# Four 32-row groups instead of two 64-row halves for the query-key sums of a linear-attention and gated-MLP block

## The chip, the cores and the metric

The kernel runs on one core of one Trainium2 chip. The metric is the device time of one execution in microseconds (us); several executions are timed and their median is given. One further kind of execution is recorded by the hardware profiler, and all views of the profile come from it. The engines are PE (matmul; PEld are its weight loads), DVE (vector), ACT (scalar), POOL (GpSimd) and SP, which here issues most DMAs.

## The reference

Input `x` is 2048 rows of 640. The rows are normalised (mean and variance over 640), and the result `xn` goes through two branches whose outputs are added to `x`:

```python
# branch A: linear attention, 32 heads of width 20
q, k, v = split(xn @ wqkv)
pq, pk = q @ w_phi[h], k @ w_phi[h]                      # per head, 20 x 20
phi_q = concat(softmax(pq), softmax(-pq))                # 40 features a head
phi_k = concat(softmax(pk), softmax(-pk))
kv  = sum over rows of phi_k^T v                         # 40 x 20 a head
z   = sum over rows of phi_k
o   = (phi_q @ kv) / (phi_q . z + 1e-6)
A   = o @ wo
# branch B: gated MLP, F = 1536
B   = (silu(xn @ w1) * (xn @ w3)) @ w2
out = x + A + B
```

## The kernel before, in words

The rows are worked in 16 row tiles of 128 and in 4 chunks of 4 tiles. `h`eads lie 20 columns apart, so 640 columns are five groups of 128.

**Order of work.** Each step is an operation of a planner (`Plan`, lines 12 to 83): an engine, an estimated duration, what it depends on, which ring buffer it takes or frees. PE's operations keep the order of the code; for DVE, ACT, POOL and SP the planner picks, among the next 80 of each engine, the one that by its estimates can start first. The resulting order is written out once; on the chip each engine then runs its list in that order, held only by semaphores. Rings have fixed numbers of buffers; `bank` is six PSUM banks that all products share, `kv` two further banks, first the accumulators of the key sums and later buffers of the query-key sums.

**First part (to about 139 us).** `LN` normalises the rows of a chunk: POOL computes `rstd` (lines 316, 317) from the statistics of four tiles (lines 301, 305), DVE applies it tile by tile (line 347, `ln_apply`), SP stores `xn` and loads it back transposed as `xnT` (lines 381, 386). An apply or a statistic is pinned behind a given DVE instruction by `order_after`, so it can't run ahead of it. For chunks 2 and 3 `LN` is called at tiles 4 and 8; its four applies wait in the list `applies`, and each following call of `GU` takes one, pinned behind that call's `gs`. `K(t)` makes key features: two products (line 442), four exponentials on ACT (`ek`, line 488), the sums and reciprocals on DVE (`ks`, `kr`, lines 497 and 506), then `phik`, the positive half on DVE and the negative half on POOL (line 514). `V(t)` makes the values, `KV(t)` adds ten products of one tile to `kva` and `kvb` (line 533). `fill` places gated-MLP units `GU` between them: two products of five 512-column matmuls (line 611), `th` on ACT (627), `gs` on DVE (632), `up` on ACT (650), their product `hT` on POOL (655). A `bank` of the first product is free when `gs` is done.

**Hand-over.** After the last `KV`, `kv_evac` (lines 662 to 677) writes the masked sums into two tables `kvr[sgn]` with four DVE products of 64 rows and 420 elements (line 669): rows 0 to 63 hold the features of heads 0 to 15, rows 64 to 127 those of heads 16 to 31; a 64-row group touches four heads, 88 columns.

**Second part.** `Q(c, g)` makes the query products of a chunk (line 689) and both exponentials (`eq`, line 704). `RT` makes the query-key sums: for a row tile and one sign, five steps of two matmuls, one on rows 0 to 63 and one on rows 64 to 127 of the array, 88 columns each (line 743). Three such units form one run (`RT(b)`), eleven runs in all; a unit writes two banks, and two of three units use the `bank` ring. ACT copies them to `rt` (line 759). `ATT(pair)` turns two tiles into attention outputs on DVE (`m` to `ca`, lines 784 to 789; `om`, lines 805 and 815), `OT(pair)` stores them (`od`, line 837) and loads them transposed (`oT`, line 845). `O(t)` adds, for a row tile, `hT @ w2` (line 871) and `oT @ wo` (line 877) in one bank; DVE adds the input (`res`, line 889), SP stores the output (line 894). The runs 3 to 10 lie in the middle of a tile's w2 products.

Of the kernel before, what the change touches and what calls it, by code (L numbers as in the profile page):

```python
# [86 lines left out]
def kernel(  # L87
# [33 lines left out]
    h0 = [64 * j // Dh for j in range(10)]  # L121
    g0 = [P * g // Dh for g in range(NQ)]

    x2 = A_x[0]
# [30 lines left out]
    vaug = [acts.tile([P, H, Dh + 1], bf, name=f"vaug{i}") for i in range(4)]  # L155
    kvr = [acts.tile([P, NQ, 4 * HC], bf, name=f"kvr{i}") for i in range(2)]
    kva, kvb = (kvpool.tile([P, 512], f32, name=n, tag="kv", bufs=2) for n in ("kva", "kvb"))
# [45 lines left out]
    band2 = consts.tile([P, 20], bf, name="band2")  # L203
    mask = consts.tile([P, NQ, 4], bf, name="mask")
    hmask = consts.tile([P, NQ, GH], bf, name="hmask")
# [45 lines left out]
    def kv_constants():  # L251
        make_band(band2[0:64, :], 20)
        make_band(band2[64:128, :], 20)
        for g in range(NQ):
            b = 4 - (64 * g - Dh * h0[g]) // 4
            nc.gpsimd.tensor_copy(out=mask[:, g, :], in_=band2[:, b : b + 16 : 5])
        for kv in kvr:
            nc.gpsimd.tensor_copy(out=kv[:].rearrange("p g (h c) -> p g h c", c=HC)[:, :, :, HC - 1], in_=mask[:])
# [10 lines left out]

    plan = Plan(dict(bank=6, five=4, half=2, pair=4, rt=4, kv=2, th=3, gs=3, up=3, hT=3, big=4))  # L270

# [6 lines left out]
    def dve_us(n, x=1):  # L278
        return 0.065 + n / 960.0 / x
# [76 lines left out]

    applies = []

    def LN(c, k=None):

        ln_rstd(c)

        def al():
            xn[c] = five.tile([P, 4, D], bf, name="xn", tag="five")

        a = xn_of[c] = plan.alloc("five", al)
        if k is None:  # L370
            for i in range(4):
                applies.append(lambda k, i=i: ln_apply(4 * c + i, [a, pin_of[k]], k))
            applies.append(lambda k: LN_out(c, [apply_of[4 * c + i] for i in range(4)]))
        else:
            LN_out(c, [ln_apply(4 * c + i, [a, pin_of[k]], k) for i in range(4)])

    def LN_out(c, ds):
        a = xn_of[c]
        st = plan.op(
            "SP", 0.5,  # L380
            lambda: nc.sync.dma_start(out=xn_d[c][:].rearrange("(t p) d -> p t d", p=P), in_=xn[c][:]),
            deps=ds, frees=[a], lat=3.5,
        )

        def tr():
            pinned["xnT", c] = nc.sync.dma_start_transpose(
                out=xnT[:, :, 512 * c : 512 * c + 512], in_=xn_d[c][:]
            )

        xt = plan.op("SP", 0.5, tr, deps=[st], lat=5.0)  # L390
        for t in range(4 * c, 4 * c + 4):
            XT_of[t] = xt
# [78 lines left out]
    def K(t):  # L471
# [6 lines left out]
        def alp():  # L478
            phik_b[t] = work.tile([P, 10, 2, 64], bf, name="phik", tag="rt", bufs=4)

        ekb = plan.alloc("pair", al)
        pkb = phik_a[t] = plan.alloc("rt", alp)
        for half in range(2):
# [63 lines left out]
    def prep(key, wT, dst, after):  # L547
# [6 lines left out]
        def columns(c, side):  # L554
            if key == "q":
                return dst[:, c, :].rearrange("p (g s f) -> p g s f", s=2, f=64)[:, :, side, :]
            return dst[:, c, 320 * side : 320 * side + 320].rearrange("p (g f) -> p g f", f=64)

        wphi_ready[key] = []

        def unit(c, side):
            def add():
                o = {}

                def fn():
                    o["ps"] = bank([P, 320], f32)
                    for n, (g, at, width, col) in enumerate(FSPANS[side]):
# [9 lines left out]
                        "ACT", act_us(320),  # L577
                        lambda: nc.scalar.copy(out=columns(c, side), in_=o["ps"][:].rearrange("p (g f) -> p g f", f=64)),
                        deps=[u], frees=[u],
# [82 lines left out]
    def kv_evac():  # L662
        for side, src in enumerate((kva, kvb)):
            for sgn in range(2):
                rows = slice(64 * sgn, 64 * sgn + 64)

                def fn(side=side, src=src, sgn=sgn, rows=rows):

                    nc.vector.tensor_mul(
                        out=kvr[sgn][64 * side : 64 * side + 64, :, :].rearrange("p g (h c) -> p g h c", c=HC)[  # L670
                            :, :, :, 0 : HC - 1
                        ],
                        in0=src[rows, 0:420].rearrange("p (g h c) -> p g h c", g=NQ, h=4),
                        in1=mask[rows, :, :, None].to_broadcast([64, NQ, 4, HC - 1]),
                    )

                kvr_of.append(plan.op("DVE", dve_us(420), fn, deps=[KV_of[NST - 1]]))

# [32 lines left out]

    def RT(b):

        units = []
        for n in range(3 * b, min(3 * b + 3, 2 * NST)):
            t, sgn = divmod(n, 2)
            pair, i = divmod(t, 2)
            if i == 0:

                def al(pair=pair, sgn=sgn):  # L720
                    rtt[pair, sgn] = work.tile([P, 2, H, HC], bf, name=f"rt{sgn}", tag="rt", bufs=4)

                rt_a[pair, sgn] = plan.alloc("rt", al)
            tag = "kv" if n % 3 == 1 else "bank"
            o = {}

            def take(o=o, tag=tag):
                for side in range(2):
                    if tag == "bank":
                        o[side] = bank([P, 352], f32)  # L730
                    else:
                        o[side] = kvpool.tile([P, 352], f32, name="rtbank", tag="kv", bufs=2)

            us = [plan.op("PE", 0.0, lambda: None, takes=tag), plan.op("PE", 0.0, take, takes=tag)]
            units.append((t, sgn, o, us))

        def fn():
            for t, sgn, o, _ in sorted(units, key=lambda u: (u[0] // 4, u[1]), reverse=True):
                c, tau = divmod(t, 4)
                for n, g in enumerate((NQ - 1, *range(NQ - 1))):  # L740
                    for side in range(2):
                        rows = slice(64 * side, 64 * side + 64)
                        nc.tensor.matmul(  # L743
                            o[side][:, 66 * g : 66 * g + 88], eqt[c, sgn][rows, g, tau * P : (tau + 1) * P],
                            kvr[sgn][rows, g, :], start=(n == 0), stop=(n == NQ - 1), skip_group_check=True,
                        )

        assert all(len(eq_of[t // 4, sgn]) == NQ for t, sgn, _, _ in units)
        deps = kvr_of + [x for u in units for x in eq_of[u[0] // 4, u[1]] + u[3]]
        u = plan.op(  # L750
            "PE", len(units) * pe_us(NQ, 88) + 0.2, fn, deps=deps,
            frees=[eq_a[t // 4, sgn] for t, sgn, _, _ in units],
        )
        for t, sgn, o, us in units:
            pair, i = divmod(t, 2)
            for side in range(2):

                def ev(o=o, sgn=sgn, side=side, pair=pair, i=i):
                    nc.scalar.copy(  # L759
                        out=rtt[pair, sgn][:, i, 16 * side : 16 * side + 16, :].rearrange("p h c -> p (h c)"),  # L760
                        in_=o[side][:],
                    )

                rt_of.setdefault(pair, []).append(
                    plan.op("ACT", act_us(352), ev, deps=[u, rt_a[pair, sgn]], frees=[us[side]])
                )

    o_of = {}

    def ATT(pair):  # L770
        box = {}

        def v(sgn):
            return rtt[pair, sgn][:].rearrange("p t h c -> p (t h) c")

# [24 lines left out]
        def om(sgn, c, i):  # L800
# [8 lines left out]

            return plan.op("DVE", dve_us(D), fn, deps=[a, ob[sgn]], frees=[rt_a[pair, sgn]])  # L810

# [167 lines left out]
    def fill(us):  # L979

        nonlocal gi, owed
        owed += us
        while owed > 1.1 and gi < limit:
            GU(*gus[gi], modes(gi))
            for _ in range(min(len(applies), 2 if len(applies) == 2 else 1)):
                applies.pop(0)(("g", *gus[gi]))
            gi += 1
            owed -= 2.16
        if gi == limit:
            owed = 0.0  # L990
# [9 lines left out]
    for t in range(NST):  # L1000
        K(t)
        if 1 <= t <= 8:
            fetch(7 + t, t)
        if t == 4 or t == 8:
            LN(t // 4 + 1)
        fill(1.95)
# [30 lines left out]
    Q(1, 3)  # L1037
    Q(1, 4)
    fill(2.2)
    RT(2)  # L1040
    ATT(1)
    OT(1)
    fill(4.4)
    bursts = 3
    late = {
# [3 lines left out]
    for i in range(NST // 2):  # L1049
# [3 lines left out]
        if nxt < NST // 2:  # L1053
            if nxt % 2 == 0:
                residual(nxt // 2)
            fill(2.2)
            last = (4 * nxt + 3) // 3
            for n, b in enumerate(range(bursts, last + 1)):
                mids[n].append(lambda b=b: RT(b))
            bursts = last + 1  # L1060
        if i == 5:
            fill(100)
        O(2 * i, mids[0])
        if mids[0] and not mids[1]:
            ATT(nxt)
            OT(nxt)
        fill(2.2)
# [55 lines left out]
```

## Time and profile before

| what | us |
|---|---|
| median of 6 executions | 277.93 (277.46 to 278.98) |
| the profiled execution, its own time | 278.79 |
| its span | 277.1 |
| PE busy in the span | 269.3 |
| DVE, ACT, POOL busy | 170.6, 149.6, 94.0 |
| PE, line 743 (320 matmuls) | 10.6 busy, about 203 ns each |
| ACT, line 759 (64 copies of 352 columns) | 27.5 busy, about 507 ns each |
| DVE, line 669 (4 products of 420 elements) | 2.4 busy, about 595 ns each |

The span is the time from the first to the last instruction of the profiled execution; 1.7 us lie around it. Matmuls are pipelined, so their busy times overlap and a busy PE is not PE at its peak: the distance from one start to the next tells more. In a timeline line stand the start, the length from the first start to the last end of the merged instructions, engine, source line, operation, output and inputs, shapes, count, and in brackets the idle time before it with what ended it. PE's idle time there counts from the modelled end of a matmul, which lies about 0.16 us behind the point at which the next could have started.

### The profile page before, as it was taken

Reading aid. Unit: us, or ns where it says so; the run is one execution under the profiler, and the core shown is the slowest. Engines: PE = TensorE matmul, PEld = TensorE weight load, DVE = VectorE, ACT = ScalarE, POOL = GpSimd, SP = SyncE. Lnnn points to the kernel's source line nnn. Section 1 sums busy time; section 2 is a strip of 40 time slices with the busy share of each in tenths; the row PEclk is TensorE's granted clock in tenths of the full one; section 3 lists DMA queues with packets and bytes.
Section 4 is the critical chain, followed back from the end, with each engine's and each line's share of the span. In section 5 each row is a group of like instructions: output and inputs, shape, how many; then the busy total and the mean of one; then the engine's idle time right before and its main releaser. Section 6 shows DMA issues by size and latency. Waiting matters only on the chain.

```text
span 277.1 us, 5180 instructions
## 1 busy us (share of the span) xinstructions
PE 269.3 (97%) x2031; PEld 160.7 (58%) x2031; DVE 170.6 (62%) x300; ACT 149.6 (54%) x326; POOL 94.0 (34%) x103
## 2 busy tenths in 40 slices
PE   7999999999999899999998999999999999999996
PEld 2645555555665466557544566665665566457775
DVE  5515899979977863757446995179428227519221
ACT  3668676665666576667789643544253444550000
POOL 6224557765665546455410310001111101540000
PEclk9999999999999999999999999999999999999999
DMA  7999627800460033000400324323320710300501
GB/s 202 316 285 308 197 99 171 303 2 0 133 153 0 2 115 76 2 0 2 119 0 2 87 64 136 73 89 110 105 55 27 170 68 2 110 8 26 142 24 50
DMA packets 44904, 26.57 MB, mean 96 GB/s; under 512 B 26448, under 2 KB 44880, under 8 KB 44880
## 3 DMA queue, kind: packets, MB, share of 16 engines
q1 hardware_dynamic: 44448, 25.97, 33.2%
q8 instruction: 16, 0.26, 0.4%
q10 hardware_dynamic: 432, 0.28, 0.4%
q14 instruction: 8, 0.07, 0.1%
HBM read 12.81 MB, written 7.21 MB: 72 GB/s over the span
## 4 chain that ended last, share of the span: by engine, by line
PE 86%; DVE 4%; ACT 3%; POOL 2%; issue 2%; DMA 1%; SPq 0%; POOLq 0%
PE bank L611 34%; PE bank L871 18%; PE bank L442 14%; PE bank L877 7%; PE bank L689 7%; ACT rt L759 1%; POOL phik L514 1%; PE bank L743 1%; DMA xg<-in_A_x_dram 1%; PE bank L568 1%; PE kvb L533 1%; PE kva L533 1%; DVE gs L632 1%; ACT eq L704 1%; POOL rstd L317 1%
## 5 line engine op out<-in xcount | busy, mean ns | idle before, releaser
L611 PE MATMUL bank<-xnT,w 128*128 128x512 bf16 x480 | 109.6, 379 | 1.4 <-DVE gs L632 0.8
L655 POOL TENSOR_TENSOR hT<-gs,up 128x512 bf16<-128x512 bf16 x48 | 56.3, 1174 | 140.5 <-DVE gs L632 60.8
L611 PEld LDWEIGHTS <-w 128*128 128x128 bf16 x480 | 46.7, 98 | 52.4 <-issue 1.6
L871 PE MATMUL bank<-w,hT 128*128 128x320 bf16 (+2 forms) x396 | 56.5, 295 | 0.6 <-DVE gs L632 0.4
L632 DVE SCALAR_TENSOR_TENSOR gs<-th,bank 128x512 bf16<-128x512 bf16 x48 | 32.5, 678 | 26.6 <-ACT th L627 26.2
L871 PEld LDWEIGHTS <-hT 128*128 128x128 bf16 x396 | 37.6, 98 | 16.5 <-issue 0.6
L627 ACT ACTIVATE th<-bank 128x512 bf16<-128x512 f32 x48 | 29.2, 609 | 29.0 <-PE bank L611 29.0
L650 ACT ACTIVATE up<-bank 128x512 bf16<-128x512 f32 x48 | 29.0, 605 | 24.5 <-PE bank L611 24.5
L442 PEld LDWEIGHTS <-xnT 128*128 128x128 bf16 x320 | 31.0, 100 | 14.5 <-issue 0.8
L704 ACT ACTIVATE eq<-bank 128x512 bf16<-128x512 f32 x40 | 21.8, 628 | 21.1 <-PE bank L689 21.1
L889 DVE TENSOR_TENSOR res<-bank,xr 128x320 bf16<-128x320 f32 (+2 forms) x33 | 15.4, 477 | 27.6 <-PE bank L877 27.6
L497 DVE TENSOR_REDUCE ks<-ek 128x64 f32<-128x1280 bf16 x16 | 23.6, 1475 | 13.0 <-ACT ek L488 12.9
L514 POOL TENSOR_TENSOR phik<-ek,kr 128x640 bf16<-128x640 bf16 x16 | 28.8, 1798 | 6.1 <-ACT th L627 2.5
L442 PE MATMUL bank<-wv,xnT 128*128 128x320 bf16 x160 | 25.4, 309 | 0.5 <-DVE gs L632 0.5
L488 ACT ACTIVATE ek<-bank 128x320 bf16<-128x320 f32 x64 | 23.1, 436 | 4.0 <-PE bank L442 3.7
L877 PE MATMUL bank<-wo,oT 128*128 128x320 bf16 (+2 forms) x165 | 24.7, 295 | 0.0
L442 PE MATMUL bank<-wkphi,xnT 128*128 128x320 bf16 x160 | 24.3, 299 | 0.0
L689 PE MATMUL bank<-xnT,wqphi 128*128 128x512 bf16 x100 | 23.5, 379 | 0.4 <-ACT eq L704 0.4
L514 DVE TENSOR_TENSOR phik<-ek,kr 128x640 bf16<-128x640 bf16 x16 | 22.3, 1397 | 1.1
L759 ACT CAST rt<-bank 128x352 bf16<-128x352 f32 x42 | 17.8, 509 | 6.5 <-PE bank L743 5.4
L877 PEld LDWEIGHTS <-oT 128*128 128x128 bf16 x165 | 15.9, 98 | 5.9
L784 DVE TENSOR_TENSOR m<-rt,rt 128x64 f32<-128x64 bf16 x8 | 4.0, 505 | 21.8 <-ACT rt L759 21.8
(60 smaller groups left out, 201.7 us busy)
## 6 DMA issues: line engine op xcount, KB each, us to landing
w<-in_B_w_dram SPq DMA_DIRECT2D x8, 480.0 KB, 6.3
xr<-in_A_x_dram SPq DMA_DIRECT2D x4, 640.0 KB, 5.5
od<-om SPq DMA_DIRECT2D x8, 320.0 KB, 2.3
out_dram<-res SPq DMA_DIRECT2D x15, 160.0 KB, 1.8
xnd<-xn SPq DMA_DIRECT2D x3, 640.0 KB, 3.2
w<-in_B_w_dram SPq DMA_DIRECT2D x1, 1920.0 KB, 8.5
xg<-in_A_x_dram SPq DMA_DIRECT2D x10, 160.0 KB, 3.3
wv<-in_A_wqkv_dram SPq DMA_DIRECT2D x2, 400.0 KB, 5.4
```

The costliest lines, as they stand in the source:

```text
L442: nc.tensor.matmul(o["ps"][:], xnT[:, c, t * P : (t + 1) * P], w[:, c, 320 * half : 320 * half + 320], start=(c == 0), stop=(c == KD - 1),)
L497: nc.vector.reduce_sum(out=box["s"][:].rearrange("p a h -> p (a h)"), in_=box["ek"][:].rearrange("p a (h d) -> p (a h) d", d=Dh), axis=AX.X,)
L514: phik_ins[t] = eng.tensor_mul(out=phik_b[t][:, :, sgn, :], in0=box["ek"][:, sgn, :].rearrange("p (h d) -> p h d", d=Dh), in1=box["r"][:, ...
L611: nc.tensor.matmul(o["ps"][:], w[:, k, fi * P : (fi + 1) * P], xs[:, k, :], start=(k == 0), stop=(k == KD - 1))
L627: nc.scalar.activation(out=box["th"][:], in_=og["ps"][:], func=AF.Tanh, scale=0.5)
L632: pinned["g", c, fi] = nc.vector.scalar_tensor_tensor(out=box["gs"][:], in0=box["th"][:], scalar=1.0, in1=og["ps"][:], op0=ALU.add, op1=AL ...
L650: nc.scalar.activation(out=box["up"][:], in_=ou["ps"][:], func=AF.Copy, scale=0.5)
L655: lambda: nc.gpsimd.tensor_mul(out=hT[c][:, fi, :], in0=box["gs"][:], in1=box["up"][:]),
L689: nc.tensor.matmul(o["ps"][:], wqphi[:, k, g * P : (g + 1) * P], xnT[:, k, c * 512 : (c + 1) * 512], start=(k == 0), stop=(k == KD - 1),)
L704: nc.scalar.activation(out=eqt[c, sgn][:, g, 0:512], in_=o["ps"][:], func=AF.Exp, scale=1.0 - 2.0 * sgn)
L871: nc.tensor.matmul(o["ps"][:], hT[c][:, fi, ti * P : (ti + 1) * P], w2[:, fi, lo:hi], start=(fi == 0), stop=False,)
L877: nc.tensor.matmul(o["ps"][:], oT[c][:, k, ti * P : (ti + 1) * P], wo_of[0][:, k, lo:hi], start=False, stop=(k == KD - 1),)
```

## The change

Three things are changed together.

*Query-key sums.* The query features are permuted so that 32 rows of the array hold features of eight heads: four groups of rows, each with 160 features in five steps of 32. A step then touches two or three heads, so 44 or 66 columns instead of 88. `RT(t)` handles one row tile with both signs: 2 x 5 x 4 = 40 matmuls, four banks (two `bank`, two `kv`), four copies of 352 columns as before. There are 16 runs instead of 11, and one lies in the w2 products of every tile from 0 to 11. The tables `kvr` have three heads a step instead of four and are written by 16 DVE products of 32 rows and 126 elements.

*Ring `rt`.* It has two buffers of double size instead of four: a key-feature tile and an `rt` tile each hold two row tiles (with both signs).

*Normalised rows.* The list `applies` is gone. `LN` is called at tiles 5 and 9, and its four applies are pinned behind the `phik` of that tile.

```diff
+    qh = [(0, 2), (1, 3), (3, 2), (4, 3), (6, 2)]
-    kvr = [acts.tile([P, NQ, 4 * HC], bf, name=f"kvr{i}") for i in range(2)]
+    kvr = [acts.tile([P, NQ, 3 * HC], bf, name=f"kvr{i}") for i in range(2)]
...
-        make_band(band2[0:64, :], 20)
-        make_band(band2[64:128, :], 20)
+        for q in range(4):
+            make_band(band2[32 * q : 32 * q + 32, :], 20)
...
-    plan = Plan(dict(bank=6, five=4, half=2, pair=4, rt=4, kv=2, th=3, gs=3, up=3, hT=3, big=4))
+    plan = Plan(dict(bank=6, five=4, half=2, pair=4, rt=2, kv=2, th=3, gs=3, up=3, hT=3, big=4))
...
-        if k is None:
-            for i in range(4):
-                applies.append(lambda k, i=i: ln_apply(4 * c + i, [a, pin_of[k]], k))
-            applies.append(lambda k: LN_out(c, [apply_of[4 * c + i] for i in range(4)]))
-        else:
-            LN_out(c, [ln_apply(4 * c + i, [a, pin_of[k]], k) for i in range(4)])
-
-    def LN_out(c, ds):
-        a = xn_of[c]
+        ds = [ln_apply(4 * c + i, [a, pin_of.get(k)], k) for i in range(4)]
...
         def alp():
-            phik_b[t] = work.tile([P, 10, 2, 64], bf, name="phik", tag="rt", bufs=4)
+            two = work.tile([P, 2, 10, 2, 64], bf, name="phik", tag="rt", bufs=2)
+            phik_b[t], phik_b[t + 1] = two[:, 0], two[:, 1]
...
-                return dst[:, c, :].rearrange("p (g s f) -> p g s f", s=2, f=64)[:, :, side, :]
+                return dst[:, c, :].rearrange("p (g q f) -> p q g f", q=4, f=32)[:, 2 * side : 2 * side + 2]
...
     def kv_evac():
-        for side, src in enumerate((kva, kvb)):
+        for q in range(4):
+            src = (kva, kvb)[q // 2]
             for sgn in range(2):
-                rows = slice(64 * sgn, 64 * sgn + 64)
...
+                for odd in range(2):
+                    m = 5 * (q % 2) + odd
+                    j, rows = m // 2, slice(64 * sgn + 32 * (m % 2), 64 * sgn + 32 * (m % 2) + 32)
+                    n, heads = 3 - odd, 2 + odd
+                    at = 8 * q + qh[odd][0] - h0[5 * (q // 2) + j]
...
+                    kvr_of.append(plan.op("DVE", dve_us(126), fn, deps=[KV_of[NST - 1]]))
...
+        us = [plan.op("PE", 0.0, take(q), takes="bank" if q < 2 else "kv") for q in range(4)]
...
+            for sgn in (1, 0):
+                for g in (NQ - 1, *range(NQ - 1)):
+                    head, n = qh[g]
+                    for q in range(4):
+                        rows = slice(32 * q, 32 * q + 32)
+                        at = 176 * sgn + HC * head
                         nc.tensor.matmul(
-                            o[side][:, 66 * g : 66 * g + 88], eqt[c, sgn][rows, g, tau * P : (tau + 1) * P],
-                            kvr[sgn][rows, g, :], start=(n == 0), stop=(n == NQ - 1), skip_group_check=True,
+                            o[q][:, at : at + HC * n], eqt[c, sgn][rows, g, tau * P : (tau + 1) * P],
+                            kvr[sgn][rows, g, 0 : HC * n], start=(sgn == 1 and g == NQ - 1),
+                            stop=(sgn == 0 and g == NQ - 2), skip_group_check=True,
                         )
...
+        for q in (2, 3, 0, 1):
+            def ev(q=q):
+                nc.scalar.copy(
+                    out=rtt[pair][:, :, i, 8 * q : 8 * q + 8, :].rearrange("p a h c -> p a (h c)"),
+                    in_=o[q][:].rearrange("p (a x) -> p a x", a=2),
+                )
...
             GU(*gus[gi], modes(gi))
-            for _ in range(min(len(applies), 2 if len(applies) == 2 else 1)):
-                applies.pop(0)(("g", *gus[gi]))
...
-        if t == 4 or t == 8:
-            LN(t // 4 + 1)
+        if t == 5 or t == 9:
+            LN((t + 3) // 4, t)
...
     Q(1, 4)
+    RT(2)
     fill(2.2)
-    RT(2)
+    RT(3)
     ATT(1)
...
-            last = (4 * nxt + 3) // 3
-            for n, b in enumerate(range(bursts, last + 1)):
-                mids[n].append(lambda b=b: RT(b))
-            bursts = last + 1
+            for n in range(2):
+                mids[n].append(lambda t=2 * nxt + n: RT(t))
...
         O(2 * i, mids[0])
-        if mids[0] and not mids[1]:
-            ATT(nxt)
-            OT(nxt)
```

## The prediction

> **What bounds the kernel now.** I read the page's busy table first, then its chain, then the timeline of PE wherever that shows a gap.
>
> ```profile
> PE 269.3 (97%) x2031; PEld 160.7 (58%) x2031; DVE 170.6 (62%) x300; ACT 149.6 (54%) x326; POOL 94.0 (34%) x103
> PE 86%; DVE 4%; ACT 3%; POOL 2%; issue 2%; DMA 1%; SPq 0%; POOLq 0%
> ```
>
> PE sets the time, at a granted clock of 1.0 all through. Busy time of pipelined matmuls overlaps, so I use steps (start to start): ten 512-column products take 2.16 us in the chain, 216 ns each; twelve of 320 take 1.63 us, 136 each. What PE loses is a start later than that. First, the normalised rows:
>
> ```profile
> 59.89 2.32 PE L611 MATMUL bank<-xnT,w 128*128 128x512 bf16 x10
> 62.72 1.52 PE L442 MATMUL bank<-wv,xnT 128*128 128x320 bf16 x10 [0.51 <-DVE gs L632]
> ```
>
> Ten steps from 59.89 end at 62.05; the next product starts at 62.72: 0.67 us lost, waiting for gs. On DVE:
>
> ```profile
> 59.93 0.21 DVE L305 BATCH_NORM_AGGREGATE mv<-stats 128x2 f32<-128x12 f32 x1
> 61.62 0.45 DVE L347 TENSOR_SCALAR xn<-xg,mv,rstd 128x640 bf16<-128x640 bf16 x1 [1.48 <-POOL rstd L317]
> 61.98 0.68 DVE L632 SCALAR_TENSOR_TENSOR gs<-th,bank 128x512 bf16<-128x512 bf16 x1
> ```
>
> The first normalised row of chunk 2 stands ahead of that gs and waits 1.48 us for POOL's rstd. Chunk 3 does the same:
>
> ```profile
> 89.81 1.52 PE L442 MATMUL bank<-wkphi,xnT 128*128 128x320 bf16 x10
> 92.09 2.10 PE L611 MATMUL bank<-xnT,w 128*128 128x512 bf16 x9 [0.77 <-DVE gs L632]
> ```
>
> Ten steps of 136 end at 91.17: 0.92 us lost. Second, the query-key sums:
>
> ```profile
> 141.66 0.38 PE L689 MATMUL bank<-xnT,wqphi 128*128 128x512 bf16 x1
> 141.97 0.37 PE L743 MATMUL rtbank<-kvr,eq 64*128 64x88 bf16 x10
> 142.18 0.56 PE L743 MATMUL bank<-kvr,eq 64*128 64x88 bf16 x20
> 142.67 0.60 PE L689 MATMUL bank<-xnT,wqphi 128*128 128x512 bf16 x2
> ```
>
> Ten take 0.20 us: pairs on the two 64-row halves at a step of 39 ns. Going in, 141.66 + 0.216 = 141.88 against 141.97: 0.095 us. Coming out, 142.18 + 10 x 0.039 = 142.57 against 142.67: again about 0.095. So a run costs 0.19 us beside its matmuls, eleven runs 2.1 us, and 160 pairs 6.3 us. Third, behind four runs PE waits for banks:
>
> ```profile
> 146.33 1.02 PE L689 MATMUL bank<-xnT,wqphi 128*128 128x512 bf16 x4 [0.44 <-ACT eq L704]
> ```
>
> By the same steps these waits are 0.51 us here, 0.69 behind the run of 150.93, 0.26 behind that of 158.43 and 0.48 behind that of 187.10; another 0.19 is lost going into the run of 150.93. From 142 to 155 ACT works without a pause (eq, rt, th, up).
>
> **Normalised rows.** All four of a chunk now follow phik of tile 5 (tile 9) on DVE; rstd's inputs end with tile 4 (8), so the 1.48 us wait goes, and with it 0.67 + 0.92 = 1.59 us of PE. Late next is the gs behind the four. Without the wait I lay DVE out from 60.14 by its rows: gs 0.68, ks 1.48 (ek ends at 60.85), gs, kr 0.55, phik 1.41 to 65.3, stats and mv 1.1, four applies of 0.45 to 68.2, or 69.3 if one meets a POOL product (the apply at 65.39 took 1.10), then gs until 68.9 to 70.0. Its bank, taken at 63.4, is due seven allocations on, at 69.46: 0 to 0.5 us lost. Chunk 3, alike with no stats, 0 to 0.8. I take 0.45 for both: **-1.15 us** (-1.6 to -0.3). The store and transpose of xn keep their place: the last apply ended at 70.25 before; chunk 2 is first read at 82.07.
>
> **The run.** 640 matmuls replace 320; four groups have steps of 44, 44, 66, 44, 66 columns, ten steps a row tile. Through 512 and 88 columns (216 and 39 ns) goes 0.4175 ns a column + 2.3, so 20.7 and 29.9 ns: 0.244 us a row tile if four groups overlap as two do. The shortest full step shown is 36 ns (80 columns, in the 0.16 us of L568 x3): 0.36 us. At the present 19.6 ns a matmul, no gain from four groups, 40 take 0.78. In the single records of the first run the second pair's loads start at 141.984 and .988 and their matmuls at 142.012 and .015, 28 ns later; I take 28 for the narrow steps, 30 for the wide: 0.288 us, and 0.19 to enter and leave as now, 16 times instead of 11.
>
> The Trainium skill, "TensorEngine Tiling (Array Packing)", section "Instruction Overhead", speaks against the change: about 60 cycles a matmul whatever its columns, so do not take the factor from a side already small. By it 44 columns count as 60; my line makes that 27.4 ns and an estimated 0.284 us a row tile, against 0.244 by the line alone. No run here shows a step under 80 columns.
>
> **kvr.**
>
> ```profile
> 138.80 1.20 DVE L669 TENSOR_TENSOR kvr<-kva,mask 64x420 bf16<-64x420 f32 x2 [4.00 <-PE kvb L533]
> 140.03 1.21 DVE L669 TENSOR_TENSOR kvr<-kvb,mask 64x420 bf16<-64x420 f32 x2
> 141.27 0.69 DVE L632 SCALAR_TENSOR_TENSOR gs<-th,bank 128x512 bf16<-128x512 bf16 x1
> ```
>
> Four products of 0.596 end at 141.24, under PE's GU and query product (until 141.88). Sixteen of 126 elements replace them. Rows of 420 (596 ns) and 512 elements (678) give 1.04 ns an element and 0.15 fixed, so 0.28 each and, by the 0.61 spacing here, 0.30 from start to start: 4.85 us, done at 143.65. Where DVE overlaps its products (0.816 long, 0.73 apart on L805) it would be 0.20 and 142.0; I keep 0.30, the row of this very line. Waiting behind them are gs (its bank is free at 144.3, needed at 145.1) and the first run, which starts at 143.70, 1.73 us later.
>
> The skill's "VectorE: DVE Perf Modes", section "Two Vector instructions with no wait between them", holds an instruction until its forerunners end when a start quadrant changes; each of the sixteen changes one, so by it too 0.30 stands, not 0.20.
>
> **From there to the first wo product.** ACT: rt takes 0.345 a piece, eq 0.48. Run 0 at 143.70 to 143.95, its four rt 144.2 to 145.6, eq of two products to 147.5, run 1's rt to 148.95; then DVE's ATT(0), 1.0 us later than now (148.00). Now it ends at 154.11, and the store (2.3) and transpose (3.8) land oT at 160.24, with PE there at 161.01. Then: 155.1 (154.6 if a gs moves behind), 160.7 to 161.2. PE: queries to 148.8, run 2, GU to 151.4, run 3 at 151.6 (its bank, run 2's rt, is late by 0.1), two GU to 156.3, 1.63, run 4, 1.63: at wo by 160.0. So the bank waits go (1.65 us), but 1.7 is paid for kvr and the rest at oT: start about 160.95 against 161.01, **-0.05 us** (-1.4 with kvr at 0.20 and no wait; +0.5 with ATT later).
>
> **After it.** Seven runs of now, 20 units x 0.196 + 7 x 0.19 = 5.25, against eleven of 0.478 = 5.26. A run takes two of the ring's six banks instead of four, so the 0.48 at 188 goes: **-0.48** (-0.97 at 0.244 a run, +0.3 at 0.36).
>
> **The end.** Pair 7's last run moves from tile 10 to tile 11, in present times 252.84 to 253.1; rt to 254.75, ATT(7) 5.6 + 0.8 for two res to 261.2, store 2.35, transpose 3.7: 267.3, needed at 268.7 (wo of tile 14, now at 268.39). The cover is 1.4 us; **+0.1**.
>
> At nothing: four more selects of 0.2 us on POOL, which idles from 5.3 to 11.4 us; phik tiles in pairs, since an even tile's write waits for KV of three tiles earlier, done on PE before that tile's K; the permuted query columns. The words speak of a query product ahead of the last key sums: Q(0, 0) is there already, and nothing moves.
>
> **Sum:** -1.15 - 0.05 - 0.48 + 0.1 = -1.6 us on the profiled execution's 278.79 (span 277.1 and 1.7 around it), 277.2. That run is 0.86 above the median of 277.93, so **276.3**.
>
> **Rivals.**
> - *Loads of the four groups go one after another.* For it: two loads took 28 ns above, 14 each; 40 are 0.56 us a row tile. Against: pairs overlap cleanly now. Eleven later runs cost 11 x 0.27 = 3.0 more, 0.5 more at oT (runs 0 and 1 are on that chain): +3.5, **279.8**, slower. From 0.41 us a run (1.6 / 13 more than 0.288) it decides.
> - *Four rows at once stall PE as the wait did.* Losing 1.4 instead of 0.45: 277.3; with the end's cover gone (1 us) instead, 277.3 too: no change.
> - *Everything overlaps:* 0.244 a run, kvr at 0.20, no wait at oT, no stall at rows: -1.59 - 1.4 - 0.97 = -3.96, **274.0**.
>
> **Numbers.** Forecast 0.42 and all overlapping 0.14 are faster; no change 0.24; serial loads 0.20. 0.3% is 0.83 us, about what a measurement of this kernel can tell from no change. The range takes in the forecast's own bounds and leaves out half of serial loads (0.78 us a run, near 283, among it: it needs four groups to gain nothing where two gain all) and half of full overlap: 274.5 to 279.6.
>
> **What would show it.** Run length in PE's timeline (0.24, 0.29, 0.56) and its edges (0.095); kvr ending near 143.6; no gap behind rows at 62 and 91; wo of tile 0 waiting for oT. A run over 0.41 us, or gaps over 1 us at the rows, makes the forecast wrong.

## The result and the profile after

The changed kernel takes **276.52 us** (median; 276.32 to 278.37), the kernel before 278.35 (277.41 to 279.95) in the same sessions: a ratio of 0.9948 [0.9934, 0.9962], so 1.45 us less by the ratio of the means (1.06 to 1.84); the medians lie 1.83 apart. The profiled span went from 277.1 to 274.8. The busy line and the shares of the chain of waits:

```profile
PE 267.0 (97%) x2351; PEld 158.5 (58%) x2351; DVE 170.6 (62%) x312; ACT 150.1 (55%) x326; POOL 95.2 (35%) x107
PE 85%; DVE 8%; DMA 3%; ACT 3%; issue 1%
```

320 more matmuls, and PE is busy for 2.3 us less. Neither that nor the span's 2.3 is the change's doing alone. The first GU product starts at 15.01 us in the profile of before, at 13.74 in that of after. Of the lines on PE's chain ahead of it none was changed; POOL makes five and five selects for the bands there instead of three and three, and is done with them by 6.4 us. What differs is the step of PE's first products: in the records of before the value products follow each other at 267 ns until 10.1 us and at 136 ns from 10.3 us on; in after all go at 136 ns. The two chains show it as means, fifteen products at 215 ns and ten at 153:

```profile
7.93 3.23 PE bank L442 x15
```

```profile
8.38 1.53 PE bank L430 x10
```

So from here on I measure from the first GU product to the last matmul: **259.18 us before, 258.13 after, -1.05**. A second profile of before (below) gives 259.19. Since the start moves the time of one execution of either kernel by over 1 us, the timed executions of both lie in bunches: 15 of 21 of the changed kernel at 276.32 to 276.88 (median 276.48), 20 of 47 of the kernel before at 277.41 to 277.70 (median 277.52), the rest later. These two medians are 1.04 apart, as the traces are; the rest of the difference of the overall medians is that more executions of the changed kernel started early. Whether the change makes an early start more frequent, or 21 executions happened to have more of them, wasn't tested.

Where the 1.05 lies. The stretches run from the first GU product, with the steps of the prediction (216 ns, 136 ns):

| us after the first GU product | before | after | gain since the last entry in this column |
|---|---|---|---|
| last KV product done, first table product starts | 123.79 | 122.56 | 1.23 |
| last table product ends | 126.23 | 127.43 | |
| ATT(0) starts | 132.99 | 132.93 | |
| wo of tile 0 starts | 146.00 | 145.16 | -0.39 |
| last matmul | 259.18 | 258.13 | 0.21 |

ATT(0), the first of them before and after:

```profile
148.00 0.27 DVE L784 TENSOR_TENSOR m<-rt,rt 128x64 f32<-128x64 bf16 x1 [6.04 <-ACT rt L759]
```

```profile
146.67 0.27 DVE L781 TENSOR_TENSOR m<-rt 128x64 f32<-128x64 bf16 x1 [4.78 <-ACT rt L756]
```

It waits for ACT's copies in both, and the 1.23 us that PE had gained are all but gone there.

The rows. PE of the changed kernel around the two places where it waited:

```profile
58.62 2.32 PE L602 MATMUL bank<-xnT,w 128*128 128x512 bf16 x10
60.78 1.52 PE L430 MATMUL bank<-wv,xnT 128*128 128x320 bf16 x10
```

Ten steps of 216 ns from 58.62 end at 60.78, where the next product starts: no gap. At chunk 3:

```profile
95.61 1.52 PE L430 MATMUL bank<-wkphi,xnT 128*128 128x320 bf16 x10
97.32 1.89 PE L602 MATMUL bank<-xnT,w 128*128 128x512 bf16 x8 [0.19 <-DVE gs L623]
```

Ten of 136 end at 96.97, so 0.35 us are lost. DVE shows why, and shows the tables too:

```profile
94.21 2.46 DVE L348 TENSOR_SCALAR xn<-xg,mv,rstd 128x640 bf16<-128x640 bf16 x4
96.59 0.68 DVE L623 SCALAR_TENSOR_TENSOR gs<-th,bank 128x512 bf16<-128x512 bf16 x1
...
136.30 2.42 DVE L665 TENSOR_TENSOR kvr<-kva,mask 32x126 bf16<-32x126 f32 x8 [4.07 <-PE kvb L524]
138.73 2.44 DVE L665 TENSOR_TENSOR kvr<-kvb,mask 32x126 bf16<-32x126 f32 x8
```

Four rows stand ahead of a gs for 2.46 us, and that gs ends 0.35 too late. In the single records the first of the four takes 1.39 us, beside the negative half of phik on POOL (from 93.56, 1.85 long), and the others 0.44 each; four of 0.44 would have ended 0.95 earlier, in time. The sixteen table products take 4.88 us, 0.30 from start to start.

The first run and the first wo product, on PE:

```profile
139.47 0.19 PE L742 MATMUL bank<-kvr,eq 32*128 32x44 bf16 x2
...
141.23 0.33 PE L742 MATMUL rtbank<-kvr,eq 32*128 32x44 bf16 x6 [0.89 <-DVE kvr L665]
...
156.56 1.80 PE L868 MATMUL bank<-w,hT 128*128 128x320 bf16 x12
158.91 1.26 PE L874 MATMUL bank<-wo,oT 128*128 128x320 bf16 x8 [0.55 <-DMA oT<-od]
```

Run 0 begins at 139.47 with the groups whose tables are ready and stops until 141.23 for the last one: it is stretched from 0.31 to 2.05 us. Twelve steps from 156.56 end at 158.19; oT comes 0.72 later. The other runs stand undisturbed, but for run 3, which loses 0.48 because one of its matmuls waits for a bank that ACT has still to empty:

```profile
149.72 0.18 PE L742 MATMUL rtbank<-kvr,eq 32*128 32x44 bf16 x1 [0.18 <-ACT rt L756]
```

An undisturbed one:

```profile
183.77 1.25 PE L868 MATMUL bank<-w,hT 128*128 128x320 bf16 x8
184.95 0.19 PE L742 MATMUL bank<-kvr,eq 32*128 32x44 bf16 x2
...
185.36 1.80 PE L868 MATMUL bank<-w,hT 128*128 128x320 bf16 x12
```

183.77 + 8 x 0.136 = 184.86, and the run starts at 184.95: 0.095 to enter. From 184.95 to 185.36 are 0.41 us, about 0.31 of it the run and 0.095 to leave.

### The profile page after: what moved, and what is told of

Same layout as the page of the kernel before. It is cut to its first block, busy times and chain, and to the rows that moved or that the text cites. A ratio compares the mean times of both kernels' runs of the same rounds, so it can differ in the third digit from the quotient of the medians.

```text
span 274.8 us, 5825 instructions
## 1 busy us (share of the span) xinstructions
PE 267.0 (97%) x2351; PEld 158.5 (58%) x2351; DVE 170.6 (62%) x312; ACT 150.1 (55%) x326; POOL 95.2 (35%) x107
## 4 chain that ended last, share of the span: by engine, by line
PE 85%; DVE 8%; DMA 3%; ACT 3%; issue 1%
PE bank L602 33%; PE bank L868 18%; PE bank L430 14%; PE bank L874 8%; PE bank L689 6%; DVE kvr L665 1%; DMA oT<-od 1%; PE bank L742 1%; DVE xn L348 1%; PE bank L559 1%; ACT rt L756 1%; DVE om L802 1%; PE kvb L524 1%; PE kva L524 1%; DVE stats L302 1%
## 5 line engine op out<-in xcount | busy, mean ns | idle before, releaser
L646 POOL TENSOR_TENSOR hT<-gs,up 128x512 bf16<-128x512 bf16 x48 | 56.9, 1187 | 137.0 <-DVE gs L623 89.6
L868 PE MATMUL bank<-w,hT 128*128 128x320 bf16 (+2 forms) x396 | 57.2, 295 | 0.0
L430 PEld LDWEIGHTS <-xnT 128*128 128x128 bf16 x320 | 30.4, 98 | 13.8 <-ACT xnT L417 0.8
L886 DVE TENSOR_TENSOR res<-bank,xr 128x320 bf16<-128x320 f32 (+2 forms) x33 | 15.2, 467 | 24.5 <-PE bank L874 24.5
L756 ACT CAST rt<-bank 128x352 bf16<-128x352 f32 x32 | 16.0, 502 | 18.1 <-PE rtbank L742 16.0
L430 PE MATMUL bank<-wv,xnT 128*128 128x320 bf16 x160 | 24.4, 299 | 0.4 <-ACT xnT L417 0.4
L505 DVE TENSOR_TENSOR phik<-ek,kr 128x640 bf16<-128x640 bf16 x16 | 21.3, 1333 | 0.9
L781 DVE TENSOR_TENSOR m<-rt 128x64 f32<-128x64 bf16 x8 | 2.2, 272 | 28.8 <-ACT rt L756 28.8
```

The source lines that it names most:

```text
L430: nc.tensor.matmul(o["ps"][:], xnT[:, c, t * P : (t + 1) * P], w[:, c, 320 * half : 320 * half + 320], start=(c == 0), stop=(c == KD - 1),)
L505: phik_ins[t] = eng.tensor_mul(out=phik_b[t][:, :, sgn, :], in0=box["ek"][:, sgn, :].rearrange("p (h d) -> p h d", d=Dh), in1=box["r"][:, ...
L646: lambda: nc.gpsimd.tensor_mul(out=hT[c][:, fi, :], in0=box["gs"][:], in1=box["up"][:]),
L868: nc.tensor.matmul(o["ps"][:], hT[c][:, fi, ti * P : (ti + 1) * P], w2[:, fi, lo:hi], start=(fi == 0), stop=False,)
```

## The experiments

My theory after the result: the gain is the rows' alone; four groups are no shorter in all than two halves, because the tables' 1.7 us take back what shorter runs and more banks give. The rival: the four groups gain by themselves, and the rows little. Medians are compared with the kernel before in the same session; "by the trace" is the stretch from the first GU product to the last matmul against after's 258.13 or before's 259.18.

### The rows alone, and the runs alone

`e1_rows` is the kernel before with the changed `LN` (no list of postponed applies, as in the diff of the change) and its calls:

```diff
...
-        if t == 4 or t == 8:
-            LN(t // 4 + 1)
+        if t == 5 or t == 9:
+            LN((t + 3) // 4, t)
```

> The kernel before with the change's normalised rows alone (called at tiles 5 and 9, four applies behind phik of that tile; runs and tables as before). Theory (the gain is the rows): PE's two losses of 0.67 and 0.92 us at the rows give way to 0 to 0.5, the rest of the trace stays as it was, and the time falls by 1.2 us (0.9 to 1.6) against the kernel before: about 277.1 where that one has 278.35. Rival (the gain is the four groups): no change, within 0.3 us.

277.09 us against 278.05: 0.9956 [0.9936, 0.9975]. By the trace -1.24. The place of the 0.67 us:

```profile
61.32 1.52 PE L429 MATMUL bank<-wv,xnT 128*128 128x320 bf16 x10
```

The product has no wait, and at chunk 3 0.35 us are left, as in after. The waits behind four runs are there as before (0.51, 0.19, 0.69, 0.26, 0.48). `e2_runs` is the reverse: the changed kernel with the old `LN`, its list and its calls at tiles 4 and 8.

> The changed kernel with the normalised rows put back (list, tiles 4 and 8); four groups, sixteen runs and sixteen table products stay. Theory: the waits for rstd of 0.67 and 0.92 us are back; from the first run to the end the trace is that of the changed kernel, which there is 0.2 us slower than the kernel before (0.4 lost up to wo of tile 0, 0.2 won behind it), so 0.2 us slower than the kernel before, 0 to 0.5. Rival (the four groups gain): 1 us faster than the kernel before.

278.83 us: 1.0021 [1.0002, 1.0041]. By the trace +0.65 against before, above the 0 to 0.5 expected, and 0.35 of it lies at the rows: the gaps that were 0.67 and 0.92 are 1.02 and 0.94 here.

```profile
62.69 0.57 PE L443 MATMUL bank<-wv,xnT 128*128 128x320 bf16 x3 [0.86 <-DVE gs L636]
```

The wait for rstd is as long as it was. The 0.35 come from one product on DVE, the positive half of phik 31.5 us after the first GU product: it takes 1.82 us here and 1.48 in before, and all that stands behind it is later by that (the last section has its cause). The wo product of tile 0 waits 0.82 us for oT, which it didn't before. The two runs settle the main point: the rows bring the whole gain, and the four groups none, with the old rows (they lose the other 0.30 of the 0.65) or with the new ones, where they lose 0.19 (258.13 in after, 257.94 in `e1_rows`). That they gain nothing is clear from this. The size of the loss is not: each figure rests on one profile a kernel, though two profiles of before agree within 0.02, and the timed medians can't tell so little.

### What the tables' sixteen products cost

`e6_kvr4` makes four of the sixteen; the other entries of the tables hold ones, so the output isn't the reference's.

```diff
+            nc.gpsimd.memset(kv[:], 1.0)
...
-        for q in range(4):
+        for q in (3,):
```

> The changed kernel with four of the sixteen table products (heads 24 to 31 alone); the tables of the other heads hold ones, so twelve products are left out and the output of those heads is not the reference's. The tables end 3.6 us earlier, ahead of PE. Theory after the first four runs (the tables hold up run 0, but ACT is next in line there): PE's 1.74 us at run 0 go; run 0's copies start behind the eq of product (1,0), at 140.7 instead of 141.74, so ATT(0) and oT come 1.1 us earlier, and wo of tile 0 still waits 1.0 to 1.4: 1.1 us (0.8 to 1.4) faster than the changed kernel. Rival (the tables alone set this stretch): 1.74 + 0.71 = 2.4 us faster.

275.43 us: 0.9905 [0.9868, 0.9942], by the trace -1.30 against after. Run 0 doesn't wait, ATT(0) starts 1.17 us earlier, and wo of tile 0 still waits 0.58 us for oT. So the tables cost 1.3 us, not the 2.4 of the rival: behind them ACT is next in line. Its row there, from `e6_kvr4`:

```profile
140.51 0.46 ACT L757 CAST rt<-bank 128x352 bf16<-128x352 f32 x1
```

The copies of run 0 follow two exponentials (from 139.54) without a pause, and so does all else until 147; in the changed kernel ACT stood still for 1.07 us there:

```profile
139.58 1.08 ACT L704 ACTIVATE eq<-bank 128x512 bf16<-128x512 f32 x2 [0.42 <-PE bank L689]
141.74 0.45 ACT L756 CAST rt<-bank 128x352 bf16<-128x352 f32 x1 [1.07 <-issue]
```

### Other work on PE while the tables are made

If run 0 waits for the tables, PE can make query products meanwhile. The changed kernel has Q(1, 0), run 0, then Q(1, 1). `e3_order` puts two more ahead, `e7_order2` one:

```diff
 e3_order
-    RT(0)
     Q(1, 1)
     Q(1, 2)
+    RT(0)
+    Q(1, 3)
...
-    Q(1, 3)
```

```diff
 e7_order2
     Q(1, 0)
+    Q(1, 1)
     RT(0)
-    Q(1, 1)
     Q(1, 2)
```

> The changed kernel with the query products (1,1) and (1,2) ahead of run 0, and (1,3) between runs 0 and 1, (1,4) behind run 1. Theory (the sixteen table products set a chain: tables, run 0, run 1, ATT(0), store, transpose, wo of tile 0): PE's wait of 1.74 us at run 0 goes, ACT has one pair of eq between the runs' copies instead of two, so ATT(0) starts 0.9 us earlier and oT lands 0.9 us earlier; wo of tile 0 waits 0.0 to 0.2 instead of 0.71, and the time falls by 0.7 us (0.4 to 1.0) below the changed kernel. Rival (PE's products alone set the time there): the 1.74 us at run 0 are gained whole, 1.7 us. Second rival (wo of tile 0 waits for something other than this chain): the wait moves there and nothing is gained.

276.99 us: 0.9961 [0.9935, 0.9987]; by the trace -0.16 against after, where 0.7 was expected. Run 0 doesn't wait (0.31 us), and yet ATT(0) starts where it did. I missed this; ACT shows why:

```profile
139.61 3.24 ACT L704 ACTIVATE eq<-bank 128x512 bf16<-128x512 f32 x6 [0.42 <-PE bank L689]
142.74 0.46 ACT L756 CAST rt<-bank 128x352 bf16<-128x352 f32 x1
```

Six exponentials, four of them of the two products moved ahead, stand in ACT's queue before run 0's copies, which start at 142.74; in after they start at 141.74. The wait has moved to ACT's queue, and from there to runs 1 and 2, which wait for banks and last 0.99 and 1.12 us instead of 0.31, and to wo of tile 0, which waits 1.28 us for oT.

> The changed kernel with query product (1,1) ahead of run 0, (1,2) between runs 0 and 1, (1,3) and (1,4) behind run 1. In the first reordering ACT worked off six eq ahead of run 0's copies, in the changed kernel it stood idle from 140.66 to 141.74 and had four eq between the runs. Theory (ATT(0) waits for ACT's list ahead of it, tables second): with two eq in the idle time and two between the runs ATT(0) starts 0.95 us earlier, at 145.7; wo of tile 0 waits 0.7 to 0.9 less against the changed kernel where PE is also 0.6 or more earlier at it, and the time falls by 0.9 us (0.6 to 1.2) below the changed kernel. Rival (wo of tile 0 is held by something else): within 0.2 us of the changed kernel.

276.53 us: 0.9917 [0.9893, 0.9941]; by the trace -1.07, ATT(0) 0.96 us earlier.

```profile
141.06 2.17 ACT L704 ACTIVATE eq<-bank 128x512 bf16<-128x512 f32 x4 [0.42 <-PE bank L689]
143.24 0.45 ACT L756 CAST rt<-bank 128x352 bf16<-128x352 f32 x1
```

Four exponentials, and the copies follow at once: one product ahead fills ACT's pause, and two overfill it. Four take 2.17 us, 0.54 each, and a query product has two: 1.1 us of ACT, which is the pause that it fills (1.07).

### The rest of the wait at the rows

`e4_both` was meant to join `e3_order` with rows that go one by one behind gs again, as before, but only from tiles 5 and 9 on. `e8_rows2` calls `LN` at tiles 4 and 8, lets two gs pass, and puts two rows behind each of the next two.

```diff
 e8_rows2
...
+        if k is None:
+            applies.extend([lambda k: None] * 4)
+            for i in range(4):
+                applies.append(lambda k, i=i: ln_apply(4 * c + i, [a, pin_of[k]], k))
...
+            for _ in range(min(len(applies), 3 if len(applies) == 3 else 2)):
+                applies.pop(0)(("g", *gus[gi]))
...
-        if t == 5 or t == 9:
-            LN((t + 3) // 4, t)
+        if t == 4 or t == 8:
+            LN(t // 4 + 1)
```

> As the run with the reordered query products, and the normalised rows of chunks 2 and 3 one behind each gs as before the change, but called at tiles 5 and 9. Theory (what stood in PE's way was the wait for rstd, and in the changed kernel four applies in a row): neither is left, the 0.35 us at 96.8 go too, and the time is 0.35 us (0.1 to 0.5) below that run, about 1.0 below the changed kernel. Rival (the call's place matters, the row of four does not): equal to that run within 0.1.

284.39 us: 1.0193 [1.0162, 1.0224]. Missed by far. The rows end so late that the transposed chunk isn't there when the keys of tile 8 need it:

```profile
83.79 2.85 PE L443 MATMUL bank<-wkphi,xnT 128*128 128x320 bf16 x10 [3.47 <-DMA xnT<-xnd]
```

PE stands for 3.5 us, and the ten products after it take 2.85 us where ten take 1.52 elsewhere: the granted clock is 0.5 from 82.85, still within the pause, until 89.68. The keys of tile 12 wait for another 1.95 us. So the slack of the rows has two ends: a row too soon holds up a gs, and a row too late the transpose.

> The changed kernel with another place of the normalised rows: called at tiles 4 and 8, two gs passed by, then two applies behind each of the next two gs. Theory: rstd is there when the first apply comes (no wait as before the change), two applies in a row delay a gs by 0.9 us, which the banks cover, and the store leaves as early as in the kernel before, so none of the 3.6 us that tile 8's key product waited in the version called at tiles 5 and 9: the 0.35 us at 96.8 go, 0.35 us (0.1 to 0.5) faster than the changed kernel. Rival (any apply ahead of a gs costs PE): 0 to 0.5 us slower than the changed kernel.

276.51 us: 0.9941 [0.9919, 0.9963]; by the trace -0.40 against after, as the 0.35 at chunk 3 asked. There the steps follow each other without a gap:

```profile
96.78 1.52 PE L444 MATMUL bank<-wkphi,xnT 128*128 128x320 bf16 x10
98.14 1.24 PE L616 MATMUL bank<-xnT,w 128*128 128x512 bf16 x5
```

### Both mends together

`e9_best` is `e7_order2` with the rows of `e8_rows2`.

> Both: the query products in the second order and the rows in the second place. Theory: the stretches are apart (62 to 97 us, 139 to 160 us), so the gains add: 0.9 + 0.35 = 1.2 us below the changed kernel (0.7 to 1.7). Rival: as much as the better of the two alone.

**275.24 us** (274.88 to 275.70): 0.9890 [0.9862, 0.9918], the fastest of all; by the trace -1.20 against after. The singles add up to 1.47; what is missing stands at wo of tile 0, where PE now comes earlier and oT does not:

```profile
157.78 0.45 PE L888 MATMUL bank<-wo,oT 128*128 128x320 bf16 x2 [0.65 <-DMA oT<-od]
```

### What sets the length of a run

`e5_narrow` gives every step 44 columns; the third head of the wide steps is left out of the sums.

```diff
-                    head, n = qh[g]
+                    head, n = qh[g][0], 2
```

> The changed kernel with two heads (44 columns) in every step of a run; the third head of two steps in five is left out, so the output of those heads is not the reference's. Theory (a step of four matmuls has a floor near 25 to 28 ns that its loads set, whatever its columns): all steps 25 to 28 ns, the run 0.27 to 0.29 us instead of 0.31. Rival (columns set the step, 0.4175 ns each and 2.3): 21 ns a step, 0.22 to 0.23 us with the first step's 39.

278.05 us in one execution, before 277.51 beside it. A run takes 0.30 us against 0.31, a little above the 0.27 to 0.29 expected. In the records of the single matmuls the steps are 39 ns for the first, then 25, and 27 to 33 at the end; the lines of the first group show it, rounded:

```profile
172.06 0.18 PE L742 MATMUL bank<-kvr,eq 32*128 32x44 bf16 x2
...
172.09 0.18 PE L742 MATMUL bank<-kvr,eq 32*128 32x44 bf16 x2
```

44 columns are below a floor of 25 ns; by columns they would go at 20.7 (the prediction's line). In after, 66 columns take 29 to 30, on that line. By the trace this kernel is 0.34 us longer than after, and not for the runs: the transpose to oT took 4.39 us instead of 3.74, and wo of tile 0 waits 1.38 us for it. `e11_halves` keeps the 40 matmuls, but lets groups 0 and 1 do their ten steps first and then groups 2 and 3:

```diff
-            for sgn in (1, 0):
+            for h, sgn in ((0, 1), (0, 0), (1, 1), (1, 0)):
...
-                    for q in range(4):
+                    for q in (2 * h, 2 * h + 1):
```

> The changed kernel with the same forty matmuls of a run in another order: groups 0 and 1 through all ten steps, then groups 2 and 3, so twenty steps of two matmuls. Theory (the floor is that of one group: a load after the last matmul has begun, then the next matmul): a 44-column step of two stays at 25 to 28 ns, a run is 20 steps, 0.54 to 0.58 us. Rival (the floor is the rate at which the array takes instructions, about 7 ns a load and matmul): a step of two takes 21 ns at 44 columns and 30 at 66, a run 0.48 to 0.51. Second rival (loads of groups go one after another): a step of two is half of a step of four, a run stays at 0.31.

281.82 us in one execution (its first GU product starts at 17.42 us, 3.7 later than after's; by the trace 259.78, +1.65, about what eleven later runs of 0.166 more each make, 1.8). A run takes 0.476 us, less than my theory's 0.54 to 0.58 and at the lower edge of the rival's 0.48 to 0.51, but not for the rival's reason: the steps of two are still 25 to 29 ns, as those of four are. What saves time is the hand-over:

```profile
166.59 0.36 PE L742 MATMUL bank<-kvr,eq 32*128 32x44 bf16 x14
166.78 0.19 PE L742 MATMUL rtbank<-kvr,eq 32*128 32x44 bf16 x2
...
166.88 0.36 PE L742 MATMUL rtbank<-kvr,eq 32*128 32x44 bf16 x14
```

Groups 2 and 3 (rtbank) start at 166.78, while 0 and 1 (bank) go on until 166.86, in the lines left out. So the floor is each group's own, and groups overlap across steps: a step of four groups takes what a step of two does.

### Before again

> The kernel before once more, for its start. Theory (the first 25 us differ from execution to execution, whatever the kernel, by when TensorE's full clock sets in): from the last of its early key-weight products to the last matmul 249.0 to 249.1 us as in its first profile; the stretch ahead of it anywhere from 23.8 to 25.3. Rival (the change itself shortens the start): 25.1 again, and 1.2 us of the gain are the change's start.

One execution of 277.49 us. First GU product at 13.68 us, last matmul 259.19 later: the start moves between executions of the same kernel, the rest doesn't. Its chain has ten value products in 1.53 us there, 153 ns each as in after, where the first profile of before had 215: in that one the full step set in later. The other profiles fit this: in all 13, steps at half pace end by about 5.9 us where the first GU product starts at 13.7 to 14.3, and at 9.4 to 10.4 us where it starts at 14.6 to 15.2; in `e11_halves` half pace comes back from 8.3 to 14.1 us, and it starts at 17.42.

## Why the prediction was right, step by step

The forecast of 276.3 meets 276.52, and its range holds it, but the sum behind it was 0.5 us too good: -1.6 against -1.05 by the trace. The base was low as well: the executions shown had a median of 277.93, where 47 of them have 278.35. Both errors pull the forecast down, and it meets the measured median by luck: by the trace's -1.05 that would be 277.30, and it is 0.8 lower because 15 of the 21 executions started early, against 20 of 47 of the kernel before, of which the prediction knew nothing. Its mechanism holds at the rows, at the run and at the tables; its sum is off between the tables and the first wo product. And "a granted clock of 1.0 all through" doesn't hold for the first 10 us of that profile, whose products went at 267 ns instead of 136.

- **Rows, -1.15: right.** Measured -1.23, and -1.24 alone in `e1_rows`. The forecast of 0.45 us left is 0.35, all of it at chunk 3; at chunk 2 the bank behind the four rows was due later than the gs, the favourable end of the 0 to 0.5 given. At chunk 3 the case it named came, one row beside a product of POOL. The waits that went were the whole gain.
- **The run, 0.288 us: 0.31.** Steps of 25 to 28 ns and 29 to 30 as taken, edges of 0.095 as taken; the first step of 39 ns was left out, and the last step's four matmuls come apart. `e5_narrow` shows 25 ns at 44 columns, not the line's 20.7, and `e11_halves` shows that each group pays this beside the others. The Trainium skill's "TensorEngine Tiling (Array Packing)", "Instruction Overhead", gives about 60 cycles of overhead a matmul; counting 44 columns as 60, as the prediction did, is an estimated 0.284 us a row tile, nearer to the 0.31 than the line's 0.244.
- **Tables, 4.85 us and 1.73 of wait: right** (4.88, 1.74), with some luck: the two rows it names (420 elements 596 ns, 512 elements 678) give 0.89 ns an element and 0.22 us fixed, not 1.04 and 0.15, and so 0.33 us for 126 elements. Measured are 0.28 to 0.29, which fits 1.04 and 0.15; with 0.33 the tables would have ended about 0.8 us later. The loads of the four groups go side by side; the rival with serial loads had 0.56 a run.
- **To the first wo product, -0.05: the term that failed, +0.39.** oT decides, as the prediction says, with 0.72 of wait (forecast 0.95), but it comes later. ATT(0) starts 1.17 us later relative to the tables' start than before, not 1.0. And the gs that might have moved behind ATT(0) didn't: it takes 0.60 of the chain, as in before, where I had counted on half.

The chain of waits of the changed kernel (start, length), read down from that gs: the store of od, the transpose to oT, and the product that waited for it (158.91, above).

```profile
151.79 0.60 DVE gs L623
...
152.82 2.29 DMA od<-om
...
155.12 3.74 DMA oT<-od
```

In times of before (2.50 later: 1.27 of start and 1.23 of rows) this is oT at 161.41, 0.45 later than the forecast's 160.95, and inside its bound of +0.5. `e7_order2` shows what could have been seen ahead: while run 0 waits for the tables, ACT waits too, and one query product more ahead of the run gives 1.07 us back.

- **After it, -0.48: -0.21.** The wait of 0.48 at 188 did go; eleven runs at 0.31 instead of 0.288 take back 11 x 0.022 = 0.24.
- **The end, +0.1 as a risk: 0.** No wait for oT at the last tiles.

Of the rivals, four rows at once did stall PE, for 0.35 us and not for the 1.4 that it would take to matter. "Everything overlaps" fell on all its parts but the rows: the tables' products don't overlap (0.30 apart), and the run stays above 0.244.

What stays open: why the full step sets in at another time in each execution. No run varied the start alone, and whether the change has a share in how often it is early is open too. And the end of each run is fed slowly (the last two steps' loads lie 8 ns apart in after's records); whether the instruction queue runs dry there wasn't tried.

## What to carry to other kernels

A reorganised matmul that fills the array better gains nothing where a step already costs a floor (25 ns here) and the reorganising brings sixteen small vector products to a point that the whole machine waits for; the row order that came with it made the gain. Where one engine has to wait at a hand-over, look which others stand still with it, and move ahead just as much work as the shortest of those pauses holds: one query product gained 1.07 us, two gained 0.16. And compare two profiles between two points that the change doesn't touch before the difference of their spans is believed: here the start alone made over half of the 2.3 us.

## What the runs showed of the hardware that was not expected

- Matmuls on different 32-row groups start independently of the program's order: in `e11_halves` groups 2 and 3 start at 166.785, ahead of matmuls of groups 0 and 1 that stand before them and start at 166.797 to 166.859.
- The smallest step at 32 rows is 25 ns, at 44 columns; the first step of a run, 44 columns too, takes 39.
- In `e4_both` PE had no work from 80.2 to 83.8 us, and the granted clock was 0.5 from 82.85 to 89.68: it fell 2.7 us into the pause and stayed there for 6.8 us. Pauses of 0.7 us (oT in after) and of 1.95 us (the keys of tile 12 in `e4_both`) weren't followed by a lower clock.
- A row of the apply took 0.45 us or up to 1.10 in before, and four took 2.46 in after, where four of 0.45 would be 1.8. DVE and POOL can hold each other up, and the phik product of 31.5 us after the first GU product shows it in all 13 profiles, where it meets POOL's hT. Where DVE starts 2 ns ahead or less, it takes 0.82 us and hT 1.84 (after, `e5_narrow`); where POOL starts 8 to 17 ns ahead, DVE takes 1.82 and hT 1.15 (`e2_runs`, `e8_rows2`); where POOL is 0.35 us ahead, DVE takes 1.48 (before, `e1_rows`). From the first start to the last end it is 1.83 to 1.84 us each time, nearly the shortest lengths, 0.82 and 1.15, one after the other: the two take turns, and nanoseconds decide which of them waits.
